# Attention and two expert layers in one program: where the first tile of the first layer is written in, and when the rest of w_out is decoded

## The chip, the cores and the metric

The kernel runs on one core of one Trainium2 chip. The metric is the device time of one execution, in microseconds (us). The engines are named as the profile names them: PE is TensorE, ACT ScalarE, DVE VectorE, POOL GpSimd, SP SyncE; each works through its own list of instructions, and semaphores tie the lists together.

## The reference

Three stages follow each other. The shapes are 4 batches, 8 heads, 768 positions, head size 64, so 3,072 tokens of 512 numbers, which leave the attention as `x`.

```python
# attention: 4 sink positions and a window of 128
scores = np.where(is_sink | in_window, scale * q @ k.T, -1e9)
attn = softmax(scores) @ v
# first MoE: w_in (512 x 1024), w_out (1024 x 512)
h = x @ w_in
solu = h * softmax(h)
ln = (solu - mean) / np.sqrt(var + 1e-6) * g_ln
x2 = ln @ w_out
# second MoE: 8 experts, the best one per token
e = argmax(x2 @ w_gate)
out[token] = gate[token] * (np.maximum(x2 @ w1[e], 0) @ w2[e])
```

## The kernel before, in words

**Tiles.** The attention is done in 32 units of two heads by 384 positions (`unit`, L153). Four units in a row hold all eight heads of 384 positions, which is a block of three tiles of 128 tokens; so units 0 to 3 feed tiles 0 to 2 of the first MoE, units 4 to 7 tiles 3 to 5, and so on to 24 tiles. A unit loads q and k (`a_load`), splits them into a high and a low float32r part (`a_split`: two copies on ACT at L179 and L180, two subtractions on POOL, nine copies by DMA at L187), makes six score matrices (`a_scores`: PE at L217 and L218, the mask and row maximum on DVE at L220, the exponential on ACT at L222), transposes them (`a_trans`, PE L270, ACT L271) and multiplies by v (`a_out`, PE L286 and L292). The result leaves PSUM as `bxh` (ACT, L297) and `bxl` (DVE, L298). The first three units use plain float32 and skip the split.

**The first MoE.** For each tile `m_in` makes two sums `h` of 12 matmuls each, three (L420 to L422) for each of the four 128-row chunks of w_in; chunk k reads unit k of the block. `m_act` then takes both sums through softmax and the normalisation: ACT at L437 (two), L445 (two), L448, L449 and L454, with small steps of DVE between. `m_tr` transposes (L469, ACT L472), `m_out` multiplies by w_out (L490 to L492) and writes the tile to DRAM. `moe1` (L530) has the tiles two deep: tile u goes in while tile u-2 goes out, and before the first `m_out` it asks for all of w_out (`yield ("wo", 0)`, L550).

**The weights.** w_in and w_out come as 64-bit float patterns and are decoded in 8 steps each (`decode`, L311): a DMA issued on ACT's queue (L314), two integer steps on DVE (`dt`, `dec`), two conversions on ACT (L321, and `dh` at L323), an addition on POOL (L324), a product on DVE (L325), then high and low part (ACT L362, DVE L363 for w_out). A w_out step also copies the block (ACT L366), transposes it on PE (L342, `wt`), copies it again (ACT L344, `xt`) and multiplies it by the gate weights (PE L350, `wt2`).

**PSUM.** `ps` (L78) hands out the eight banks of 128x512: three of them for the attention's `s`, `tp`, `skp` and `av`, five for the rest: `h`, `lt`, `x2`, `wt`, `wt2`, `dt`, `dh`. An `h` keeps its bank from its first matmul to its last reader, L445 of `m_act`.

**What sets the order.** Three generators are written into the program in turns: `ga` (attention), `gw` (weights) and `gm` (first MoE). First comes a loop that takes one step of the attention at a time, 110 of them (`C0`), and every sixth (`WSTEP`) one decode step: the eight of w_in first, and from step 62 on (`C1`) those of w_out.

```python
while done_x[0] < 0 or cnt_ < C0:                      # L1147
    step(ga, "a")
    cnt_ += 1
    ...
    if cnt_ % WSTEP == 0 and (wn[0] < 8 or C1 <= cnt_ and wn[0] < 16):
        step(gw, "w")
        wn[0] += 1
for _ in range(max(0, 16 - wn[0])):                    # L1155
    step(gw, "w")
    ...
```

Then a second loop (L1162) takes turns between the attention, while its written work is at most 0.7 (`RATIO`) of that of the first MoE, and one step of the first MoE; each second step of the MoE (`WSTEP2`) it takes one step of `gw`, if any is left. A unit is some 14 steps of the attention, and its output is written two units behind its scores: after 70 steps the scores of six units and the outputs of four are written, after 110 the scores of nine and the outputs of six. This written order is not yet that of the engines: the framework's scheduler goes over it and lists, for each engine, what it expects to be ready. So a matmul written later can stand earlier on PE than one written before it.

Of the kernel before, what the change touches and what calls it, by code (L numbers as in the profile page):

```python
# [37 lines left out]
XT = 21  # L38
WSB = 6
HG, HD, HSTEP, FH = 1, 5, 2, 2  # L40
C0, C1, WSTEP, WSTEP2, RATIO = 110, 62, 6, 2, 0.7
ROOM = [608, 576, 512, 416, 384, 320, 288, 128]
CAPS = [-(-n // 128) * 128 for n in ROOM]
NBLK = sum(CAPS) // 128
# [8 lines left out]
def body(ctx, tc, a):  # L53
# [476 lines left out]
    def moe1(nt):  # L530
        yield ("in", 0)
        m_x(0)
        for t in range(-LA, nt):
            u = t + LA
            if u < nt:
                yield from m_in(u, 0)
                if u + 1 < nt:
                    if (u + 1) % 3 == 0:
                        yield ("in", (u + 1) // 3)
                    m_x(u + 1)  # L540
            if t >= 0 and t != nt - 2:
                yield from m_tr(t)
            if u < nt:
                yield from m_in(u, 1)
                tin[0] = u + 1
                m_act(u)
            if t == nt - 3:
                yield from m_tr(t + 1, True)
            if t == 0:
                yield ("wo", 0)  # L550
            if t >= 0:
                yield from m_out(t, 128 * t, m_route(t - 1, tok_i[:, t - 1:t]) if t else ())
            if t == TE + 1:
                yield ("head", 0)
# [99 lines left out]
    def open_w():  # L654
        pool2["w"] = c_ctx.enter_context(tc.tile_pool(name="w2p", bufs=1, side="right"))
# [146 lines left out]
    def head():  # L802

        wq = []
        plan_head()
        for _ in range(HG):
            yield 0
        for c in range(4):
            w_fetch(0, 1, c)
        with tc.issue_after(loaded[-1].ins):  # L810
            load_ids(0, 0, HEAD)
        for _ in range(HD):
            yield 0
        x_gather(0, 0, HEAD)
        parts = [(which, c) for which in (1, 2) for c in range(4)]
        for n, p in enumerate(parts):
            if p == (2, 3):
                while not early_t:
                    yield 0
            if p[0] == 2 and p not in wq:  # L820
                w_fetch(0, *p)
            tc.keep_in_program_order(w_high(0, *p))
            if n < 3:
                w_fetch(0, 2, n)
                wq.append((2, n))
            yield 0
            tc.keep_in_program_order(w_low(0, *p))
            yield 0
        while len(late) <= XT:
            yield 0  # L830
        with tc.issue_after(late[XT].ins):
            for _ in x_trans(0, 0, HEAD):
                pass
# [275 lines left out]
    def weights():  # L1109
        yield from load_w_in()  # L1110
        yield from load_w_out()

    ga, gm, gw = attention(), moe1(NT), weights()
# [3 lines left out]
    def step(g, name):  # L1117

        y = hold.pop(name, None)
        if y is None:  # L1120
            y = next(g, None)
        if y is None:
            return None
        if isinstance(y, tuple):
            kind, b = y
            if kind == "x":
                done_x[0] = b
            elif kind == "head":
                assert not a_open
                open_w()  # L1130
                gh[0] = head()
            elif kind == "wo":
                while step(gw, "w") is not None:
                    pass
            elif kind == "w" and tin[0] < b:
                hold[name] = y
                return 0
            elif kind == "in":
                if done_x[0] < b:
                    hold[name] = y  # L1140
                    return 0
                done_in[0] = b
            return 1e-6
        return max(y, 1e-6)

    cnt_, wn = 0, [0]
    while done_x[0] < 0 or cnt_ < C0:  # L1147
# [4 lines left out]
        if cnt_ % WSTEP == 0 and (wn[0] < 8 or C1 <= cnt_ and wn[0] < 16):  # L1152
            step(gw, "w")
            wn[0] += 1
    for _ in range(max(0, 16 - wn[0])):  # L1155
        step(gw, "w")
        wn[0] += 1
    ta = tm = 0.0
    mcnt = 0
    gh = [None]  # L1160
# [81 lines left out]
```

## Time and profile before

| what | before |
|---|---|
| median of 3 runs | 844.85 us (836.87 to 855.21) |
| the profiled execution, its own time | 840.65 us |
| its span, first to last instruction | 838.9 us |
| PE busy | 787.2 us, 94% of the span |
| ACT, DVE, POOL busy | 495.1, 489.7, 383.4 us |
| mean granted clock of PE | 0.983 of full |

The profile is of one execution. Its span leaves out 1.75 us of its own time. A busy PE is pipelined: a matmul's row overlaps the next, so the price of one in a row of many is the distance between starts. Windows give, for a stretch of the span, how long each engine was busy, and the clock that PE was granted. A wait names the engine that waited, and what ended the wait.

### The profile page before, as it was taken

Reading aid. Unit: us, or ns where it says so; the run is one execution under the profiler, and the core shown is the slowest. Engines: PE = TensorE matmul, PEld = TensorE weight load, DVE = VectorE, ACT = ScalarE, POOL = GpSimd, SP = SyncE. Lnnn points to the kernel's source line nnn. Section 1 sums busy time; section 2 is a strip of 40 time slices with the busy share of each in tenths; the row PEclk is TensorE's granted clock in tenths of the full one; section 3 lists DMA queues with packets and bytes.
Section 4 is the critical chain, followed back from the end, with each engine's and each line's share of the span. In section 5 each row is a group of like instructions: output and inputs, shape, how many; then the busy total and the mean of one; then the engine's idle time right before and its main releaser. Section 6 shows DMA issues by size and latency. Waiting matters only on the chain.

```text
span 838.9 us, 15049 instructions
## 1 busy us (share of the span) xinstructions
PE 787.2 (94%) x4946; PEld 685.3 (82%) x4946; DVE 489.7 (58%) x1606; ACT 495.1 (59%) x1236; POOL 383.4 (46%) x418
## 2 busy tenths in 40 slices
PE   2667999999999999999999989999999999999996
PEld 1246878988788888888888879889988898989985
DVE  6977777787587776767675575435314242434430
ACT  4788787877568777777775464244324252544541
POOL 4877755464355455545432021157225262635531
PEclk9998899999999999999999999999999999999998
DMA  7688555677665565566420271277325253536410
GB/s 263 196 223 212 140 149 139 92 166 122 118 166 118 126 158 128 135 152 113 119 28 28 36 242 35 69 255 242 95 91 191 88 187 101 181 122 200 150 57 17
DMA packets 77383, 114.34 MB, mean 136 GB/s; under 512 B 14125, under 2 KB 53485, under 8 KB 77296
## 3 DMA queue, kind: packets, MB, share of 16 engines
q1 hardware_dynamic: 69744, 91.02, 43.1%
q0 software_dynamic: 5248, 13.88, 4.7%
q10 hardware_dynamic: 2304, 8.39, 3.2%
q8 instruction: 41, 0.67, 0.4%
q14 instruction: 46, 0.38, 0.3%
HBM read 72.22 MB, written 13.94 MB: 103 GB/s over the span
## 4 chain that ended last, share of the span: by engine, by line
PE 77%; DMA 11%; issue 4%; DVE 3%; ACT 3%; POOL 1%; POOLq 0%; SPq 0%; ACTq 0%; DVEq 0%
PE x L490 5%; PE x L492 5%; PE ht L770 5%; PE x L491 5%; PE ht L771 5%; PE ht L772 5%; PE h L420 5%; PE h L422 5%; PE h L421 5%; PE y L792 5%; PE y L791 5%; PE y L790 5%; PE av L292 4%; PE s L217 3%; PE s L218 2%
## 5 line engine op out<-in xcount | busy, mean ns | idle before, releaser
L222 ACT ACTIVATE P<-P,mx 128x272 f32<-128x272 f32 x192 | 98.7, 515 | 30.4 <-DVE mx L220 29.3
L490 PE MATMUL x<-woh,lh 128*128 128x256 f32 (+1 forms) x384 | 112.2, 292 | 0.4 <-DVE ll L473 0.4
L492 PE MATMUL x<-woh,ll 128*128 128x256 f32 (+1 forms) x384 | 110.7, 289 | 0.0
L491 PE MATMUL x<-wol,lh 128*128 128x256 f32 (+1 forms) x384 | 109.7, 286 | 0.0
L220 DVE CUSTOM_DVE_ANT_0 P<-s,mk 128x272 f32<-128x272 f32 x192 | 81.0, 435 | 36.6 <-PE s L218 34.2
L694 POOL TENSOR_TENSOR wl<-wst,wh 128x1024 fp32r<-128x1024 f32 x28 | 68.3, 2438 | 64.1 <-ACT wh L688 63.9
L688 ACT ACTIVATE wh<-wst 128x1024 fp32r<-128x1024 f32 x64 | 67.5, 1058 | 47.1 <-PE ht L771 35.5
L771 PE MATMUL ht<-xel,wh 128*128 128x288 f32 (+6 forms) x288 | 90.0, 314 | 0.0
L772 PE MATMUL ht<-xeh,wl 128*128 128x288 f32 (+6 forms) x288 | 89.8, 313 | 0.0
L790 PE MATMUL y<-wh,hh 128*128 128x512 f32 x224 | 89.6, 401 | 0.0
L770 PE MATMUL ht<-xeh,wh 128*128 128x288 f32 (+6 forms) x288 | 88.5, 313 | 0.0
L792 PE MATMUL y<-wh,hl 128*128 128x512 f32 x224 | 88.1, 395 | 0.0
L791 PE MATMUL y<-wl,hh 128*128 128x512 f32 x224 | 87.6, 392 | 0.0
L694 DVE TENSOR_TENSOR wl<-wst,wh 128x1024 fp32r<-128x1024 f32 x36 | 55.6, 1552 | 50.7 <-ACT wh L688 50.7
L420 PE MATMUL h<-wih,bxh 128*128 128x512 f32 x192 | 78.8, 410 | 0.0
L421 PE MATMUL h<-wil,bxh 128*128 128x512 f32 x192 | 76.9, 401 | 0.0
L422 PE MATMUL h<-wih,bxl 128*128 128x512 f32 x192 | 76.7, 400 | 0.0
L490 PEld LDWEIGHTS x<-woh,lh 128*128 128x128 f32 x384 | 73.0, 190 | 1.3 <-DVE ll L473 0.5
L797 ACT ACTIVATE y<-y,gate 128x512 f32<-128x512 f32 x28 | 19.3, 689 | 92.8 <-PE y L792 73.5
L491 PEld LDWEIGHTS x<-wol,lh 128*128 128x128 f32 x384 | 73.1, 190 | 0.7 <-issue 0.2
L492 PEld LDWEIGHTS x<-woh,ll 128*128 128x128 f32 x384 | 73.2, 191 | 0.6 <-issue 0.3
L774 DVE SCALAR_TENSOR_TENSOR hl<-ht,hh 128x288 fp32r<-128x288 f32 (+6 forms) x80 | 38.3, 491 | 57.5 <-ACT hh L773 57.2
(229 smaller groups left out, 2067.2 us busy)
## 6 DMA issues: line engine op xcount, KB each, us to landing
wst<-w SPq DMA_DIRECT2D x64, 512.0 KB, 3.9
x_d<-xrow SPq DMA_DIRECT2D x24, 264.0 KB, 6.2
qd<-qT SPq DMA_DIRECT2D x32, 192.0 KB, 3.5
qB<-qA SPq DMA_DIRECT2D x58, 96.0 KB, 3.2
lB<-lA SPq DMA_DIRECT2D x58, 96.0 KB, 2.6
kd<-kx SPq DMA_DIRECT2D x16, 280.0 KB, 3.3
w<-w_in ACTq DMA_DIRECT2D x8, 512.0 KB, 7.5
w<-w_out ACTq DMA_DIRECT2D x8, 512.0 KB, 4.5
```

What stands on the lines that cost most here:

```text
L420: T.matmul(h, xh[k], wih[:, k, cs], start=(k == 0), stop=False)
L421: T.matmul(h, xh[k], wil[:, k, cs], start=False, stop=False)
L490: T.matmul(p[:, 0:n], lh[:, k, :], woh[:, k, c, 0:n], start=(k == 0), stop=False)
L491: T.matmul(p[:, 0:n], lh[:, k, :], wol[:, k, c, 0:n], start=False, stop=False)
L492: mm = T.matmul(p[:, 0:n], ll[:, k, :], woh[:, k, c, 0:n], start=False, stop=(k == 7))
L694: return (G if c % 2 and r else V).tensor_tensor(out=l_, in0=st_w.pop((r, which, c)), in1=raw(h_), op=ALU.subtract)
L770: T.matmul(o, wh[:, k, fs], xh(k), start=(k == 0), stop=False)
L771: T.matmul(o, wh[:, k, fs], xl(k), start=False, stop=False)
L772: T.matmul(o, wl[:, k, fs], xh(k), start=False, stop=(k == 3))
L790: T.matmul(o, hh[:, k, sl], wh, start=(k == 0), stop=False)
L791: T.matmul(o, hh[:, k, sl], wl, start=False, stop=False)
L792: T.matmul(o, hl[:, k, sl], wh, start=False, stop=(k == 7))
```

## The change

`C0` goes from 110 to 70, so the second loop begins behind the output of unit 3, some four units earlier, and the loop that wrote what was left of the 16 decode steps ahead of it is gone. With 70 steps only the first step of w_out is written in the first loop; the other seven are written in the second, one at every second step of the first MoE, all within its first two tiles.

```diff
-C0, C1, WSTEP, WSTEP2, RATIO = 110, 62, 6, 2, 0.7
+C0, C1, WSTEP, WSTEP2, RATIO = 70, 62, 6, 2, 0.7
...
             wn[0] += 1
-    for _ in range(max(0, 16 - wn[0])):
-        step(gw, "w")
-        wn[0] += 1
     ta = tm = 0.0
```

**PE behind unit 0's output.** In the fences below a row is one instruction, or several equal ones; numbers behind the names tell tiles apart, and they are counted in written order, so the same number need not be the same tile in both programs. `av_419` is unit 0's output in both. Before, from there on:

```order
L292 MATMUL av_419<-pt_310,vd_256 64x128 x2
L217 MATMUL s_456<-kA_404,qA_400 128x272
L218 MATMUL s_456<-kA_404,lA_402 128x272
L342 MATMUL wt_837<-ident_78,dec_790 128x128 x4
L217 MATMUL s_461<-kB_405,qB_401 128x272
L218 MATMUL s_461<-kB_405,lB_403 128x272
L217 MATMUL s_479<-kA_404,qA_400 128x272
L218 MATMUL s_479<-kA_404,lA_402 128x272
L217 MATMUL s_484<-kB_405,qB_401 128x272
L218 MATMUL s_484<-kB_405,lB_403 128x272
```

and with the change:

```order
L292 MATMUL av_419<-pt_310,vd_256 64x128 x2
L217 MATMUL s_456<-kA_404,qA_400 128x272
L218 MATMUL s_456<-kA_404,lA_402 128x272
L217 MATMUL s_461<-kB_405,qB_401 128x272
L218 MATMUL s_461<-kB_405,lB_403 128x272
L420 MATMUL h_817<-wih_68,bxh_441 128x512
L421 MATMUL h_817<-wil_69,bxh_441 128x512
L342 MATMUL wt_836<-ident_78,dec_790 128x128 x4
L217 MATMUL s_479<-kA_404,qA_400 128x272
L218 MATMUL s_479<-kA_404,lA_402 128x272
L422 MATMUL h_817<-wih_68,bxl_442 128x512
```

The first sum of the first tile (`h_817`) now begins right behind unit 0's output. Before, the first L420 stands behind unit 4's output. The six matmuls of the first sum that read units 0 and 1 stand before unit 2's output now, and its last behind the scores that follow unit 3's.

**PE between the outputs of unit 5 and unit 6.** `av_1086` before and `av_1243` with the change are unit 5's. Before:

```order
L286 MATMUL av_1086<-skt_849,vsk_361 128x384 x2
L292 MATMUL av_1086<-pt_874,vd_802 64x128 x2
L292 MATMUL av_1086<-pt_874,vd_802 64x256 x4
L292 MATMUL av_1086<-pt_874,vd_802 64x128 x2
L350 MATMUL wt2_1301<-wg_sb_121,xt_1299 128x8 x4
L420 MATMUL h_1361<-wih_68,bxh_441 128x512
L421 MATMUL h_1361<-wil_69,bxh_441 128x512
L422 MATMUL h_1361<-wih_68,bxl_442 128x512
L420 MATMUL h_1361<-wih_68,bxh_560 128x512
L421 MATMUL h_1361<-wil_69,bxh_560 128x512
L217 MATMUL s_1139<-kA_1071,qA_1067 128x272
```

and with the change:

```order
L286 MATMUL av_1243<-skt_856,vsk_361 128x384 x2
L292 MATMUL av_1243<-pt_916,vd_802 64x128 x2
L292 MATMUL av_1243<-pt_916,vd_802 64x256 x4
L292 MATMUL av_1243<-pt_916,vd_802 64x128 x2
L350 MATMUL wt2_1200<-wg_sb_121,xt_1146 128x8 x4
L342 MATMUL wt_1207<-ident_78,dec_1132 128x128 x4
L217 MATMUL s_1321<-kA_1228,qA_1224 128x272
L218 MATMUL s_1321<-kA_1228,lA_1226 128x272
L217 MATMUL s_1326<-kB_1229,qB_1225 128x272
L218 MATMUL s_1326<-kB_1229,lB_1227 128x272
L217 MATMUL s_1334<-kA_1228,qA_1224 128x272
L218 MATMUL s_1334<-kA_1228,lA_1226 128x272
```

Before, 48 matmuls of L420 to L422 stand between the outputs of units 5 and 6; with the change none does. Counted over PE's list, before the outputs of units 4, 5 and 6 stand 0, 12 and 60 of these matmuls in the program before, and 36, 48 and 48 in the changed one; of the eight transposes of w_out (L342) 6, 8 and 8 before, and 4, 6 and 8 in the changed one; and before unit 6's output all eight L350 groups of four stand in the program before, and seven in the changed one.

**ACT up to the copy of unit 6.** `bxh_1313` before and `bxh_1417` with the change are unit 6's. Before:

```order
L449 ACTIVATE sc_1359<-sc_1359 128x1
L222 ACTIVATE P_1136,sm_1138<-P_1136,mx_1137 128x272
L271 ACTIVATE pt_1213<-tp_1214 128x3x128
L271 ACTIVATE pt_1213<-tp_1219 128x3x128
L445 ACTIVATE h_1445,sc_1495<-e_1571,sc_1495 128x512
L445 ACTIVATE h_1497,sc_1495<-e_1571,sc_1495 128x512
L297 ACTIVATE bxh_1313<-av_1245 128x384
L454 ACTIVATE e_1426<-e_1426,sc_1359 128x1024
```

and with the change:

```order
L448 ACTIVATE sc_1179<-sc_1179 128x1
L222 ACTIVATE P_1318,sm_1320<-P_1318,mx_1319 128x272 x2
L271 ACTIVATE pt_1374<-tp_1375 128x3x128
L271 ACTIVATE pt_1374<-tp_1380 128x3x128
L449 ACTIVATE sc_1179<-sc_1179 128x1
L344 ACTIVATE xt_1261<-wt_1256 128x512
L454 ACTIVATE e_1280<-e_1280,sc_1179 128x1024
L297 ACTIVATE bxh_1417<-av_1406 128x384
```

The L454 that ends tile 0's normalisation stands behind the copy of unit 6 before; now both tile 0's and tile 1's stand ahead of it. Counted over ACT's list from the copy of unit 0 to that of unit 6, the changed program has two L454, one L448, one L449 and two L323 more, one more DMA issue (L314), and is otherwise the same, instruction for instruction.

## Rows read from the trace of the kernel before

**Rows 1.** The page: span, TensorE's busy share, and the span in 40 slices.

```profile
span 838.9 us, 15049 instructions
...
PE 787.2 (94%) x4946; PEld 685.3 (82%) x4946; DVE 489.7 (58%) x1606; ACT 495.1 (59%) x1236; POOL 383.4 (46%) x418
...
PE   2667999999999999999999989999999999999996
PEclk9998899999999999999999999999999999999998
```

**Rows 2.** Busy time by stretch; first line: the columns (PEclk: granted clock).

```profile
core 0: us, PE busy (x) PEld busy (x) DVE busy (x) ACT busy (x) POOL busy (x), PEclk, DMA share, GB/s
50.88:92.70 41.82, 32.28 (x195) 25.94 (x196) 31.70 (x97) 36.61 (x97) 31.86 (x34) 0.80 0.79 205
92.70:119.77 27.07, 26.82 (x171) 22.33 (x171) 20.75 (x70) 19.27 (x58) 14.97 (x19) 1.00 0.53 132
50.88:119.77 68.89, 59.10 (x365) 48.27 (x365) 52.45 (x166) 55.88 (x155) 46.83 (x52) 0.88 0.69 177
143.84:196.00 52.16, 52.16 (x366) 46.23 (x365) 41.31 (x151) 40.20 (x120) 25.61 (x28) 1.00 0.75 123
196.00:220.00 24.00, 20.47 (x142) 17.35 (x141) 14.16 (x53) 14.03 (x41) 11.82 (x16) 0.93 0.69 127
```

**Rows 3.** The timeline of ScalarE: copies of units 0, 4 and 6.

```profile
50.88 0.49 ACT L297 ACTIVATE bxh<-av 128x384 fp32r<-128x384 f32 x1 [1.14 <-PE s L218]
92.70 0.49 ACT L297 ACTIVATE bxh<-av 128x384 fp32r<-128x384 f32 x1
119.77 0.47 ACT L297 ACTIVATE bxh<-av 128x384 fp32r<-128x384 f32 x1
```

**Rows 4.** The timeline of TensorE: the first tile's start, before unit 5.

```profile
start us, us, engine line op out<-in xcount [idle before <-releaser]
92.58 1.06 PE L350 MATMUL wt<-wg_sb,xt 128*128 128x8 f32 x8
93.50 0.64 PE L342 MATMUL wt<-ident,dec 128*128 128x128 f32 x4
93.89 0.48 PE L420 MATMUL h<-wih,bxh 128*128 128x512 f32 x1
...
95.17 0.39 PE L420 MATMUL h<-wih,bxh 128*128 128x512 f32 x1
95.41 0.39 PE L421 MATMUL h<-wil,bxh 128*128 128x512 f32 x1
95.64 0.39 PE L422 MATMUL h<-wih,bxl 128*128 128x512 f32 x1
```

**Rows 5.** Groups by line, ScalarE, whole span; the time behind | is busy.

```profile
L454 ACT ACTIVATE e<-e,sc 128x1024 f32<-128x1024 f32 x24 | 29.7, 1239 | 11.7 <-DVE sc L453 11.7
L323 ACT ACTIVATE dh<-w 128x512 f32<-128x512 f32 x16 | 10.1, 629 | 0.0
L449 ACT ACTIVATE sc<-sc 128x1 f32<-128x1 f32 x24 | 4.7, 194 | 0.2
L448 ACT ACTIVATE sc<-sc 128x1 f32<-128x1 f32 x24 | 4.6, 192 | 0.5 <-DVE sc L447 0.3
```

**Rows 6.** Waits of ScalarE from 46 to 110 us.

```profile
engine line waited for: us in total, times, longest us
ACT woh L362 <- DVE dh L325: 3.4, 2, 2.0
ACT w L321 <- DMA w<-w_out: 3.3, 4, 1.8
```

**Rows 7.** Waits of VectorE from 46 to 110 us, same columns.

```profile
DVE dt L318 <- ACT xt L344: 2.3, 2, 1.9
```

**Rows 8.** Waits of TensorE from 119.77 us to the end, same columns.

```profile
PE s L218 <- DMA lA<-lA: 3.5, 2, 2.0
```


## The prediction

> **What bounds the kernel now.** I read the page first. PE is busy 94% of the span, and in the row of slices it is short of full only in the first four of 40, each 21 us long, and in the last; its granted clock is under nine tenths in the fourth, the fifth and the last [rows 1]. So behind some 110 us the kernel is a row of matmuls, and what the change can win or lose is decided ahead of that. The windows tell what that stretch is like [rows 2]. I set their marks at the copies of units 0, 4 and 6 on ACT, at 50.88, 92.70 and 119.77 us [rows 3], because the order of the change can be counted at the same marks. From unit 0 to unit 4 PE is busy 32.28 of 41.82 us, at a mean clock of 0.80, and ACT 36.61 of 41.82, which is 87.5%, more than any other engine. From unit 4 to unit 6 it is the other way round: PE 26.82 of 27.07 us, ACT 19.27, or 71%. From 143.84 to 196.00 PE has no gap at all: 52.16 of 52.16. The reader is to see two phases: a start in which ACT sets the pace, and PE has 9.5 us to spare, and then PE alone. The first L420 starts at 93.89 us [rows 4], where the phases meet.
>
> **What the change moves, and its price.** The matmuls of tiles 0 and 1 go from behind unit 4 into the first phase: 36 of them stand ahead of unit 4's output, where none stood. Their price is the distance of their starts, 95.17 to 95.41 to 95.64, or 0.235 us each [rows 4], so 8.5 us in all, against 9.5 us that PE stood idle there [rows 2]. At first sight that is a gain of 8.5 us. But what was taken from the second phase is not replaced: between units 4 and 6 the changed order has 12 of these matmuls in place of 60, and no other MoE work, only scores and late decode steps. So the second phase becomes one in which PE waits, and the question is when unit 6 is reached.
>
> That I take from ACT's list, since its contents between the copies of units 0 and 6 differ by so little. It was busy 55.88 us of 68.89 there [rows 2]. Added are two L454 at 1.239 us, two L323 at 0.629, one L448 at 0.192 and one L449 at 0.194 [rows 5]: 2.48 + 1.26 + 0.39 = 4.1 us, so 60.0 us. (A DMA issue more on ACT's queue I count as nothing: its own row is not busy time.) How long 60.0 us of work take depends on how well ACT is fed, for which the rows give three rates. At 100%, which no stretch shows, 60.0 us: unit 6 comes 8.9 us sooner. At the 87.5% of the first phase, 68.6 us: 0.3 us sooner. At the 81.1% of the whole stretch (55.88 of 68.89), 74.0 us: 5.1 us later. I take 87.5%, because the whole stretch from unit 0 to unit 6 now looks like the first phase did, with decode steps, scores and PE in gaps.
>
> Against that stands what PE has done by then. Ahead of unit 6's output the changed list has 12 matmuls of L420 to L422 fewer (48 in place of 60), 12 x 0.235 = 2.8 us, and one group of L350 fewer. The profile has each such group as eight rows; one takes from 92.58 to 93.50, so 0.9 us [rows 4]. Behind unit 6 PE is full, so those 3.7 us are owed. The three rates give -8.9 + 3.7 = -5.2, -0.3 + 3.7 = +3.4 and +5.1 + 3.7 = +8.8 us.
>
> The remaining edits: the seven decode steps written later are the same instructions. Before unit 4's output stand four transposes in place of six, and all eight are done by unit 6, long before the first L490, so the request for all of w_out costs nothing; were it late, the first L490 would wait with all of PE behind it. Seven loads of w_out are written later on ACT's queue; ACT waited 3.3 us for such loads, in four waits [rows 6], which is inside the 87.5%. POOL (46.83 of 68.89) and DVE (52.45) have room [rows 2]. SP's copies for the split are the same ones in a moved order, and one later stall hangs on their landing: from 196 to 220 us PE lacks 3.5 us, waiting for `lA` [rows 2, 8], and runs at a mean clock of 0.93, another 0.07 x 24 = 1.7 us. The changed program meets that place with its transfers shifted, so it can be spared the 5.2 us, meet them again, or meet them twice: I take once, and keep -5.2 and +5.2 for the range. Behind unit 31 both orders have nearly the same work left (504 matmuls of L420 to L422 are through in both), so the second MoE moves as a block.
>
> The sum is made against the profiled execution's own 840.65 us: 840.65 + 3.4 = 844.05, say 844. That execution lies 4.2 us under the median of the three runs, 844.85; by the median the sum would be 848.3. I keep 844 and let the range hold the other.
>
> **A rule for the clock.** In the first phase the clock was 0.80 with PE idle 23% of the time; in the second it was 1.00 with PE full [rows 2]. The Trainium skill ("TensorE: Matmul & The Clock Gate", section "Why this matters for your kernels") asks for no idle gaps between bursts of matmuls, as PE falls to the half level behind one. By that rule the 36 matmuls in the gaps would hold the clock at 2.4 GHz, and up to 0.20 x 41.82 = 8.4 us come back: 844.05 - 8.4 = 835.7. I do not take it, because ACT was the fuller engine in that stretch and a faster PE does not feed it more than 100%.
>
> **Rival one, a gain.** PE has matmuls between the scores, its clock stays up, scores come sooner, and ACT loses its gaps. For it: 1.14 us of waiting for PE just at the first copy [rows 3], and that the first phase was paced by nobody fully. Against it: 3.3 us of ACT's gaps were w_out loads [rows 6], and a score now stands behind matmuls that want a `bxh` just made. At ACT's limit it gives 840.65 - 5.2 = 835.4. That is also where the rule for the clock ends up, so the two share a chance.
>
> **Rival two, slower.** A sum `h` that begins behind unit 0 holds its bank until L445, behind unit 3. The first tile's two sums lie open from unit 1 to unit 3, so two of the five banks outside the attention are gone, and `dt`, `dh`, `wt` and `wt2` of each decode step take turns in three. In the rows such turns show already with five: DVE waited with `dt` for ACT's reading of `wt` 2.3 us in two waits, 1.15 each [rows 7], and ACT waited with `woh` for `dh` 3.4 us in two, 1.7 each [rows 6]. If all seven late decode steps pay both, 7 x 2.85 = 20 us fall on ACT, the engine that sets the pace: 844.05 + 20 = 864. It is slower by 2% (857.5) from 1.9 us a step on. Against it: seven steps in 68.9 us are one in 10 us, and the banks it needs are free most of that. What makes such a wait dear is what stands behind it. The Trainium skill ("PSUM — Partial Sum Buffer", section "Engine vs sequencer instructions") has the queues of ScalarE and VectorE as strictly first in, first out; by that rule each of these waits holds the exponentials and masks behind it too, and the 864 stands.
>
> **Rival three, no effect.** The order shows that the tiles do move, so the change does what it says; but with ACT at 60.0 of 65.2 us, 92%, what is won up to unit 6 and the 3.7 us owed cancel: 840.65.
>
> **How the numbers follow.** The forecast, ACT at 80 to 90%, has 0.45; rival three 0.2; rival one 0.25; rival two 0.1. Most of this lies close together: -5.2 to +8.8 us, and with the later stall once less or once more -10.4 to +14.0, so 830 to 855; the median's 4.2 us widen the upper end to 858. A difference of 2% (17 us) is about what a measurement of this kernel can tell from no change. Faster by more than that needs rival one, the spared stall and 6 us that I see nowhere: 0.04. Slower needs rival two, or the forecast's 81% with the stall met twice and more: 0.1. Within 2%: 0.86.
>
> **What would show it.** In the changed profile the first L420 should start near 52 us, behind the first copy on ACT. The seventh copy should start 68.6 us behind the first: 60 us would prove rival one, 74 or more rival two or a loss of pace. ACT should be busy 60 us between them. PE should have its gaps between the copies of units 4 and 6 now, some 9 us of them where there were 0.25 (26.82 busy, less 48 x 0.235, plus one group of L350 at 0.9 and two of L342 at 0.39 [rows 4], is 17.2 of some 27 us), and fewer ahead of unit 4. If PE is full through both phases, I am wrong about ACT. If DVE's `dt` and ACT's `dh` or `woh` wait for banks in five steps or more, rival two is at work. If the L490 of the first tile waits for `wol` or `woh`, the cover over the decode was thinner than I counted.

## The result, and the profile after

The changed kernel took 851.73 us in the median of four runs (849.26 to 855.53), the kernel before 844.07 us beside it (836.87 to 855.21): a ratio of 1.0108, interval 1.0063 to 1.0153. A later repeat on another chip gave 1.0154 (1.0127 to 1.0182). So it is 8 to 13 us slower, where the forecast was 3.4 us slower. The profiled execution, the slowest of the four, took 855.53 us, 14.9 us more than that of before. The page of the changed kernel:

```profile
span 853.7 us, 15061 instructions
...
PE 794.3 (93%) x4946; PEld 689.4 (81%) x4946; DVE 498.3 (58%) x1606; ACT 495.2 (58%) x1236; POOL 386.8 (45%) x418
...
PE   2667789999999999999999989999999999999996
PEclk9998879999999999999999999999999999999998
```

PE's fifth and sixth slices (some 85 to 128 us) were 9 and 9 and are 7 and 8 now, and the granted clock is low up to the sixth [rows 1]. Behind that PE's row is 9 but for one slice of 8 and the last, as before. The timeline of ScalarE, copies of units 0, 1, 2, 3, 4, 5 and 6:

```profile
50.40 0.49 ACT L297 ACTIVATE bxh<-av 128x384 fp32r<-128x384 f32 x1 [0.58 <-PE av L292]
58.81 0.49 ACT L297 ACTIVATE bxh<-av 128x384 fp32r<-128x384 f32 x1
74.65 0.51 ACT L297 ACTIVATE bxh<-av 128x384 fp32r<-128x384 f32 x1
85.03 0.51 ACT L297 ACTIVATE bxh<-av 128x384 fp32r<-128x384 f32 x1
104.13 0.48 ACT L297 ACTIVATE bxh<-av 128x384 fp32r<-128x384 f32 x1
116.73 0.50 ACT L297 ACTIVATE bxh<-av 128x384 fp32r<-128x384 f32 x1
131.61 0.49 ACT L297 ACTIVATE bxh<-av 128x384 fp32r<-128x384 f32 x1 [0.29 <-PE av L292]
```

Unit 0 is where it was; unit 4 came at 92.70 and comes at 104.13, unit 6 at 119.77 and now 131.61 [rows 3]. The worst piece is from unit 3 to unit 4: 19.1 us. Busy time by stretch (columns as in [rows 2]); the last row is from 30 us to the copy of unit 8:

```profile
50.40:104.13 53.73, 41.04 (x230) 31.79 (x230) 37.06 (x109) 38.31 (x103) 34.88 (x37) 0.87 0.68 173
104.13:131.61 27.48, 23.57 (x120) 18.77 (x120) 18.85 (x64) 21.44 (x60) 15.55 (x18) 0.69 0.43 114
50.40:131.61 81.21, 64.61 (x350) 50.56 (x350) 55.91 (x171) 59.76 (x161) 50.42 (x54) 0.81 0.60 153
85.03:104.13 19.10, 15.02 (x84) 12.50 (x84) 16.39 (x45) 13.29 (x36) 9.66 (x12) 0.85 0.61 150
...
30.00:163.68 133.68, 108.85 (x612) 85.37 (x613) 92.44 (x284) 97.16 (x263) 77.03 (x82) 0.89 0.57 150
```

and the same last stretch, to unit 8's copy, of the kernel before:

```profile
30.00:143.84 113.84, 95.87 (x575) 75.56 (x575) 86.60 (x268) 92.27 (x254) 77.49 (x84) 0.93 0.67 174
```

Three things are to be seen. ACT did what was counted: 59.76 us of work from unit 0 to unit 6, against 60.0 in the prediction. But it took 81.21 us over it, 73.6%. And no engine is full in either phase any more: from unit 4 to 6, where PE was full at full clock, it is busy 23.57 of 27.48 us at a mean clock of 0.69.

The last two rows give a measure for all that follows. Behind unit 8 PE is nearly full, so what counts ahead of it is the time that PE did not use, as gaps or at half clock: the stretch less busy time times mean clock. Before: 113.84 - 95.87 x 0.93 = 24.7 us. After: 133.68 - 108.85 x 0.89 = 36.8 us. The difference, 12.1 us, is most of the 14.9. Nearly all of it, 11.0 us, lies from unit 4 to unit 6: 27.48 - 23.57 x 0.69 = 11.2 us, against 27.07 - 26.82 x 1.00 = 0.25 before [rows 2]; up to unit 4 the loss grew by only 2.0 us (18.0 against 16.0).

The waits from unit 0 to 6 (us in total, times, longest), first of ScalarE, then of VectorE, then of TensorE:

```profile
ACT w L321 <- DMA w<-w_out: 5.6, 3, 2.5
ACT woh L362 <- DVE dh L325: 5.3, 3, 2.7
ACT P L222 <- DVE mx L220: 4.3, 6, 1.3
```

```profile
DVE P L220 <- PE s L218: 10.4, 6, 6.0
DVE woh L353 <- PE wt L350: 3.7, 3, 3.0
...
DVE dt L318 <- ACT dec L366: 0.7, 1, 0.7
```

```profile
PE s L217 <- DVE mx L220: 5.9, 6, 2.5
PE s L218 <- DMA lA<-lA: 2.2, 1, 2.2
```

ACT waits for DVE and for loads, DVE for PE, PE for DVE: each list waits for another. From unit 4 to unit 6 alone, where the loss lies, PE's longest waits are for DVE's masks:

```profile
PE s L217 <- DVE mx L220: 4.7, 3, 2.5
```

### The profile page after: what moved, and what is told of

The parts are those of the page before. It is cut to its first block, busy times and chain, and to the rows that moved or that the text cites. A ratio compares the mean times of both kernels' runs of the same rounds, so it can differ in the third digit from the quotient of the medians.

```text
span 853.7 us, 15061 instructions
## 1 busy us (share of the span) xinstructions
PE 794.3 (93%) x4946; PEld 689.4 (81%) x4946; DVE 498.3 (58%) x1606; ACT 495.2 (58%) x1236; POOL 386.8 (45%) x418
## 4 chain that ended last, share of the span: by engine, by line
PE 71%; DMA 10%; DVE 9%; issue 5%; ACT 3%; POOL 1%; SPq 1%; POOLq 0%; ACTq 0%; DVEq 0%
PE ht L770 5%; PE ht L771 5%; PE ht L772 5%; PE x L490 5%; PE y L792 5%; PE y L791 5%; PE y L790 5%; PE x L492 5%; PE x L491 4%; PE h L420 4%; PE h L422 4%; PE h L421 4%; PE av L292 4%; PE s L217 2%; DMA w<-w_out 2%
## 5 line engine op out<-in xcount | busy, mean ns | idle before, releaser
L490 PE MATMUL x<-woh,lh 128*128 128x264 f32 (+1 forms) x384 | 112.0, 292 | 0.4 <-DVE ll L473 0.4
L492 PE MATMUL x<-woh,ll 128*128 128x264 f32 (+1 forms) x384 | 110.3, 287 | 0.0
L491 PE MATMUL x<-wol,lh 128*128 128x264 f32 (+1 forms) x384 | 109.7, 286 | 0.0
L182 POOL TENSOR_TENSOR lA<-qd,qA 128x384 fp32r<-128x384 f32 x29 | 29.4, 1015 | 114.3 <-ACT qA L180 83.1
L420 PE MATMUL h<-wih,bxh 128*128 128x512 f32 x192 | 79.3, 414 | 0.4 <-ACT bxh L297 0.4
L422 PE MATMUL h<-wih,bxl 128*128 128x512 f32 x192 | 76.4, 401 | 0.4 <-DVE bxl L298 0.4
L490 PEld LDWEIGHTS x<-woh,lh 128*128 128x128 f32 x384 | 72.7, 189 | 1.7 <-issue 0.7
L797 ACT ACTIVATE y<-y,gate 128x512 f32<-128x512 f32 x28 | 19.3, 689 | 92.5 <-PE y L792 73.3
```

The source lines that it names most:

```text
L420: T.matmul(h, xh[k], wih[:, k, cs], start=(k == 0), stop=False)
L490: T.matmul(p[:, 0:n], lh[:, k, :], woh[:, k, c, 0:n], start=(k == 0), stop=False)
L491: T.matmul(p[:, 0:n], lh[:, k, :], wol[:, k, c, 0:n], start=False, stop=False)
L492: mm = T.matmul(p[:, 0:n], ll[:, k, :], woh[:, k, c, 0:n], start=False, stop=(k == 7))
```

## The experiments

Ratios are to the kernel before, in runs on the same chip, with their 95% intervals. "PE's loss" is the measure above, from 30 us to the copy of unit 8 (24.7 us before, 36.8 after), from each run's own windows. Where an expectation counts decode steps ahead of a unit on PE, it counts the groups of L342 and of L350 together, so 16 groups for the eight steps of w_out; 11 of them stand ahead of unit 4's output before, 8 with the change.

### Which of the two edits

The change with the loop that writes the rest of the decode put back, so that only the first tile moves (e1):

```diff
+    for _ in range(max(0, 16 - wn[0])):
+        step(gw, "w")
+        wn[0] += 1
```

> The first tile is written behind 70 steps, but all of w_out is still decoded ahead of it (the loop that wrote the rest of the decode steps is kept). In PE's list no sum of the first tile then begins before unit 4's output, as in the program before, and by unit 6 there are 72 matmuls of L420 to L422 in place of 60. Theory one (the place of the decode: steps written behind the first tiles draw the decode out, and let sums begin early that hold PSUM banks): this costs nothing, ratio to before 0.993 to 1.003, and unit 6's copy follows unit 0's by 66 to 71 us. Theory two (the attention's lead: four units less ahead, PE comes to wait for it): ratio 1.007 to 1.015, with unit 6 as early as before and PE's gaps behind it.

The late decode without the early tile (e2), the change at half the distance (e4), and the change once more (e5):

```diff
-C0, C1, WSTEP, WSTEP2, RATIO = 70, 62, 6, 2, 0.7
+C0, C1, WSTEP, WSTEP2, RATIO = 110, 108, 6, 2, 0.7   # e2
+C0, C1, WSTEP, WSTEP2, RATIO = 90, 62, 6, 2, 0.7     # e4
```

> The first tile is written behind 110 steps, as before, but only the first step of w_out is decoded ahead of it and the other seven between its steps (C0 110, C1 108, no loop). PE's list up to unit 6's output is then that of the changed kernel, nearly row for row, while the attention's written lead is that of before. Theory one (the place of the decode): ratio to before 1.006 to 1.015, unit 6's copy 76 to 82 us behind unit 0's. Theory two (the lead): ratio 0.997 to 1.004.

> The change with 90 steps in place of 70: five of the eight steps of w_out are decoded ahead of the first tile, three between its steps. The first sum begins behind unit 2's output. Theory one (the place of the decode): a third of the late decode is left, ratio 0.998 to 1.005. Theory two (the lead): half of the shorter lead, 1.004 to 1.008.

> The changed kernel once more, for a second profile and more times on the chip of the other three. Both theories: ratio to before 1.006 to 1.015. The profile of the change had unit 6's copy 81.2 us behind unit 0's, and its run was the longest of four; if that is chance, this one shows 75 to 78 us, with ACT busy some 60 us of it again.

Measured: e1 840.91 us, 1.0055 (1.0027 to 1.0084); e2 846.95, 1.0153 (1.0116 to 1.0190); e4 842.84, 1.0097 (1.0064 to 1.0131); e5 848.64, 1.0154 (1.0127 to 1.0182). PE's loss: e1 29.9, e2 32.2, e4 27.7, e5 37.1 us. The early tile alone costs a third of the loss, the late decode alone all of it; the two do not add. Of the expectations, theory one holds for e2 and both miss for e1 and e4: e4 is slower than either wanted, and e1 lies between them, though its unit 6 comes 80.7 us behind unit 0, as late as in the change. PE had done 72 matmuls of L420 to L422 by then in place of 48, so a late unit 6 is not by itself the loss. Nor does PE's loss tell all: for e4 it accounts for 3.0 of some 8 us, and where the rest lies stays open. The order of e2 tells why it is as slow as the change: up to unit 7 PE's list has the same counts of sums and decode steps ahead of each unit as the changed one (36 matmuls of L420 to L422 ahead of unit 4's output). Once the decode is written late, the sums stand as early with 110 steps as with 70, so the scheduler pulls them forward by itself. The repeat shows the same shape, 81.3 us from unit 0 to 6.

### Loads of w_out one step ahead

```diff
...
-        w = dec_p[0].tile([128, 512, 2], I32, tag="w64", name="w64", bufs=WB)
-        A.dma_start(out=w, in_=src)
+        while nf[0] < min(16, i + 2):
+            wq.append(dec_p[0].tile([128, 512, 2], I32, tag="w64", name="w64", bufs=WB)); A.dma_start(out=wq[-1], in_=srcs(nf[0])); nf[0] += 1
+        w = wq.pop(0)
...
```

> The changed kernel, with each load of a decode step issued one step ahead, so that its data lie there when ACT comes to L321; the three buffers and the order of the steps are as before. In the changed kernel ACT waited 5.6 us in three waits for w_out between units 0 and 6, up to 2.5 us at a time and 5 us in the later repeat, and the chain passes through two of them. Theory A, the chain through the queues (every wait on ACT's list holds the exponentials, the transposes' copies and the split behind it): these waits are gone, units 0 to 6 take some 76 in place of 81 us, and the kernel stands 7 to 9 us above the one before in place of 13. Theory B, the banks: ACT then waits for dh or wt in the same places, the stretch stays at 79 to 82 us and the kernel 11 to 13 us above. If it stands within 3 us of the one before, the late loads were the whole loss.

Measured: 847.00 us, 1.0110 (1.0079 to 1.0142); units 0 to 6 in 77.9 us, PE's loss 34.7. ACT's waits for w_out stay, 5.1 us in three: the edit did not move the loads. ACT's list from unit 0 on is that of the change, and the issue that came at 86.68 us comes at 85.91. So the run is nearly a repeat, and says nothing on what the loads cost.

### The banks

The kernel before with two banks held from unit 0 to unit 3 (f3; it computes four small things more, which nobody reads), and both kernels with two banks for the attention and six for the rest (`PA = 3` to `PA = 2`):

```diff
+        if not hogs and len(x_t.get(0, [])) == 1:
+            hogs = [ps("h"), ps("h")]
+            for h in hogs:
+                T.matmul(h[:, 0:128], raw(x_t[0][0][1])[:, 0:128], ident, start=True, stop=True)
+        if len(hogs) == 2 and len(x_t.get(0, [])) == 4:
+            for h in hogs:
+                V.tensor_tensor(out=const.tile([128, 1], F32, tag="hog", name="hog"), in0=h[:, 0:1], in1=raw(x_t[0][3][1])[:, 0:1], op=ALU.add)
+            hogs.append(0)
```

> The kernel before with two banks of the five outside the attention taken behind unit 0's output (two small matmuls into them) and given back behind unit 3's output (two small adds), and no first tile in between. It adds four small instructions to the computation, whose results nobody reads. Its order then has 3 decode steps in place of 11 ahead of unit 4's output, and no L420 there. Theory A, chain: with little else in the lists the bare attention steps fast, 7 us a unit or less, so units 0 to 4 take under 34 us in place of 41.8. Theory B, banks (the waits come from the two banks alone): units 0 to 4 take as long as in the changed kernel or nearly, 48 us or more, with waits for dt, dh and wt. The whole is slower than before in either case by 5 to 15 us, since eight decode steps and 46 matmuls move behind unit 4.

> The changed kernel with two of the eight PSUM banks for the attention in place of three, so six in place of five for the decode and the first MoE. Its order has all sixteen decode steps and 60 of L420 to L422 through ahead of unit 4's output. To be read against the same edit on the kernel before. Theory B, banks (the two open sums leave the decode too few): with a sixth bank the change costs little, this one is within 4 us of its control. Theory A, chain: the sums and steps still stand among the attention's instructions, this one is 8 us or more behind its control. Against the kernel before I expect it anywhere from 10 us faster (PE's matmuls fill the start) to 15 us slower (the attention with two banks steps slower, as each score waits for a mask to be done).

> The control: the kernel before with two banks for the attention and six for the rest. All sixteen decode steps are through ahead of unit 3's output in its order, and 60 of L420 to L422 ahead of unit 4's. Theory B: 5 us faster to 5 us slower than before, since here the banks were not short. Theory A: slower by 5 to 15 us, since the attention's chain loses a bank and gets more in front of it.

Measured: f3 856.21 us, 1.0214 (1.0182 to 1.0246); units 0 to 4 in 46.7 us, with `dt` waiting 0.7 us in two. Both theories missed: the bank waits were not there, and the attention was not fast, because the decode of w_in, done ahead of unit 0 before, now fell into these units too (unit 0 came at 40.98 us). With six banks 914.28 us (1.0883) after and 915.31 us (1.0924) before: the two are alike, as theory B wanted, but they are 75 us slower than the kernel before, and most of that lies behind unit 8 (PE's loss up to there is 31.7 us after and 36.3 before), so the difference between them was measured in another program. What the banks do shows in the orders: with six, all 16 groups of the decode and 60 matmuls of L420 to L422 stand ahead of unit 4's output, in place of 8 and 36 with the change and 11 and none before. Waits that look like turns for a bank (`dt` for ACT's last reading) come to 0.7 us in f3 and 0.7 us in the changed kernel.

### The split of q and k

Scores of units 3 to 6 without the split, on the changed kernel (g1) and on the one before (g2):

```diff
-NATP = 3
+NATP = 7
```

> The changed kernel with the scores of units 3 to 6 computed from the loaded q and k as they are (as units 0 to 2 are), without the split: no kA, qA, lA and none of the nine copies on SP for these units; everything else is the changed kernel. Theory A, chain: the stretch to unit 6 is long because the split (ACT, then POOL, then nine copies, then the next scores) is queued behind decode and sum work. Then units 0 to 6 take 70 us or less in place of 81, and the kernel comes to within 4 us of the one before. Theory B, banks or plain work: ACT loses eight copies (some 3 us of 59.8) and the stretch stays at 77 us or more, the kernel 8 to 13 us above the one before.

> The control for the run without the split in units 3 to 6: the same edit on the kernel before. Theory A, chain: here too the split is a part of the chain, units 0 to 4 take 36 us or less in place of 41.8, and the kernel is 3 to 8 us faster than the one before. Theory B: the start is paced by ACT's work, which loses some 3 us, and the time moves by 0 to 3 us.

Measured: g1 840.49 us, 1.0028 (1.0004 to 1.0053), PE's loss 26.3 us; g2 841.23, 1.0050 (1.0027 to 1.0073). Without split and copies most of the change's loss is gone, as theory A wanted, though unit 3 to 4 still takes 19.5 us in g1 and units 0 to 6 take 77.2, as theory B wanted. In the kernel before the same edit costs 3.5 us, against both expectations: there PE is busy 86.15 of the 87.48 us from unit 0 to 6, at a mean clock of 0.84. What a plain float32 score costs PE beside a split one was not measured by itself. So the split takes part in the loss, but is not all of it.

### More work for ACT

```diff
             A.activation(out=x, in_=p, func=AF.Copy)
+            A.activation(out=x, in_=p, func=AF.Copy)
```

> The changed kernel with the copy L366 of each w_out decode step done twice (the same result): 8 more ACT instructions of 0.6 us, 4.8 us, seven of them between units 0 and 6. If ACT's throughput paces the stretch (87.5% as in the prediction), the stretch grows by 4.2 / 0.875 = 4.8 us or more. If the stretch is paced by the serial chain of several in-order lists (theory A), it grows by about as much, 3 to 6 us, since ACT's list is one of the chain's. If the banks or PE pace it, ACT with 26% idle hides it: 0 to 1.5 us over the changed kernel's 8 to 13 us.

> The control: the kernel before with L366 done twice, 4.8 us more for ACT, nearly all of it ahead of unit 5. If ACT at 87.5% paces the start (the prediction's reading), the kernel is 4 to 6 us slower. If no single engine paces it, 1 to 4 us.

Measured: after 843.17 us, 1.0051 (1.0021 to 1.0081), before 840.58, 1.0029 (1.0000 to 1.0058). With eight ACT instructions more the changed kernel is faster than without them. From unit 0 to 6 it takes 70.0 us, and from unit 4 to 6:

```profile
99.39:120.20 20.81, 18.85 (x116) 13.97 (x117) 18.80 (x59) 19.16 (x53) 14.34 (x18) 0.92 0.55 150
```

ACT is busy 92% there and DVE 90%, where the changed kernel has 78% and 69%. The edit moves the order as well (36 matmuls of L420 to L422 ahead of unit 5's output in place of 48, and 13 groups ahead of unit 6's in place of 15), and that is the point: ACT's throughput was not what held the changed kernel at 73.6%. In the kernel before the same copies lengthen units 0 to 6 by 6.2 us, more than ACT's share at 87.5% would. But units 0 to 3, where ACT's work is the same (27.5 us against 27.9), take no longer, and all of it lies from unit 3 to 4 (17.2 us against 10.3). ACT has 4.1 us more to do there, but is busy only 75%, and these two rows of PE and DVE stand in it:

```profile
81.47 0.59 PE L218 MATMUL s<-kA,lA 128*128 128x272 f32 x1 [2.67 <-DMA lA<-lA]
82.11 0.44 DVE L220 CUSTOM_DVE_ANT_0 P<-s,mk 128x272 f32<-128x272 f32 x1 [5.39 <-PE s L218]
```

That stall will be met again below; with it this kernel is 0.3% slower (1.0029), some 2 us.

### The attention alone, and the kernel before again

The chunks of each sum in another order, so that no sum can begin before unit 3's output (e3):

```diff
-        for k in range(4):
-            T.matmul(h, xh[k], wih[:, k, cs], start=(k == 0), stop=False)
+        ks = (3, 0, 1, 2)
+        for k in ks:
+            T.matmul(h, xh[k], wih[:, k, cs], start=(k == ks[0]), stop=False)
             T.matmul(h, xh[k], wil[:, k, cs], start=False, stop=False)
-            T.matmul(h, xl[k], wih[:, k, cs], start=False, stop=(k == 3))
+            T.matmul(h, xl[k], wih[:, k, cs], start=False, stop=(k == ks[3]))
```

> The changed kernel with the four chunks of each sum of L420 to L422 in the order 3, 0, 1, 2, so that a sum can't begin before unit 3's output is there. In its order there is nothing but attention between the outputs of units 0 and 3 on PE and ACT (no decode step, no L420), and 12 matmuls and one step ahead of unit 4's. Theory A, chain: the bare attention takes 7 us a unit or less there, so units 0 to 3 come in 21 us or less (31.6 before, 34.6 after), and what is put among it lengthens it one for one. If the attention alone is already at 9 us a unit or more, its own chain sets the pace and the rest cost little in those gaps. As a whole it is the slowest of the four, 15 to 30 us above the kernel before, since decode and sums then follow one another behind unit 4.

> The kernel before, once more with a profile: whether the 41.8 us from unit 0 to unit 4, the 68.9 to unit 6 and the 24.7 us of PE time lost up to unit 8 are what it always does. I expect 41 to 46, 68 to 73 and 24 to 28 us. If they lie near the changed kernel's 53.7, 81.2 and 36.8, the profile of before was a lucky one and the comparison of the starts falls.

Measured: e3 854.51 us, 1.0206 (1.0168 to 1.0245). With nothing but attention units 0 to 3 take 23.25 us, 7.7 us each, between the two expectations; with nine groups of the decode among them (before) 31.6, with five groups and 18 matmuls (after) 34.6. So what stands among the attention does lengthen the start, by some 2 us a step of two groups (8.3 us for nine), and no engine is full even without it (PE 18.37 of 23.25 us, POOL 19.03, ACT 16.64). The kernel before, once more: 838.34 us, 1.0006 (0.9983 to 1.0029), 42.2 us to unit 4, 69.3 to unit 6, PE's loss 25.2. So its short start comes again, and so does the change's loss by this measure: 37.1 - 25.2 = 11.9 us.

### Amount or order

The late decode steps at every step of the first MoE (f5), at every fourth (f4), at every third (l2), and at every second but one step sooner (l1). For all of them the sums begin as early as in the change.

```diff
-C0, C1, WSTEP, WSTEP2, RATIO = 70, 62, 6, 2, 0.7
+C0, C1, WSTEP, WSTEP2, RATIO = 70, 62, 6, 1, 0.7     # f5; 4 in f4, 3 in l2
...
-        if mcnt % WSTEP2 == 0:
+        if mcnt % WSTEP2 == 1:                           # l1
```

> The changed kernel with a late decode step written behind every step of the first MoE in place of every second. Its order has 24 matmuls of L420 to L422 and 11 steps' transposes ahead of unit 4's output (36 and 8 in the changed kernel), and 60 and 16 ahead of unit 6's (48 and 15). If the loss comes from sums that are open while decode steps still want banks and places, it shrinks with their number: 4 to 8 us above the kernel before, units 0 to 6 in 70 to 76 us, and PE loses 2 to 5 us between units 4 and 6 in place of 11. If it comes from the matmuls being early at all, 10 us or more.

> The changed kernel with a late decode step behind every fourth step of the first MoE. Its order has 48 matmuls and 5 steps ahead of unit 4's output, 60 and 11 ahead of unit 6's, and no L420 at all between units 5 and 7. By the same reason the loss grows or stays: 13 to 20 us above the kernel before, with PE losing 12 us or more between units 4 and 8. If instead the decode is free where PE would be full, and only its number in the start counts, this one is faster than the changed kernel: 5 to 9 us above the one before.

> The changed kernel with the late decode steps written behind every second step of the first MoE as there, only one step sooner (the odd ones in place of the even). Its order has the same 3, 12, 18, 36 and 48 matmuls of L420 to L422 ahead of the outputs of units 1 to 5, and two steps more of the decode ahead of each. Theory O, the order alone (who stands directly in front of a score, a mask or an exponential on the in-order lists): with as much work in the start or more, it can lose much less; I expect units 0 to 6 in 68 to 78 us and the kernel 2 to 9 us above the one before. Theory W, amount (each sum and each decode step among the attention costs its own time): two steps more make it as slow as the changed kernel or slower, 11 to 16 us above, units 0 to 6 in 80 us or more.

> The changed kernel with a late decode step behind every third step of the first MoE (every first, second and fourth gave 3.3, 8 to 13 and 0.2 us above the kernel before). Theory O: no trend, anything from 0 to 10 us; units 0 to 6 in 65 to 78 us. A smooth law with its worst at every second step would give 5 to 9 us, and the amount of late decode in the start (theory W: fewer steps ahead of unit 4's output, 7 against 8 and 5) 4 to 8 us.

| run | ratio (interval) | ahead of unit 4: L420 to L422 / L342 and L350 groups | unit 0 to 6, us | PE's loss, us |
|---|---|---|---|---|
| before | 1 | 0 / 11 | 68.9 | 24.7 |
| the change, repeat | 1.0154 (1.0127 to 1.0182) | 36 / 8 | 81.3 | 37.1 |
| f5, every step | 1.0039 (1.0013 to 1.0065) | 24 / 11 | 72.6 | 23.6 |
| l1, one step sooner | 1.0023 (0.9994 to 1.0053) | 36 / 10 | 72.0 | 24.5 |
| l2, every third | 0.9998 (0.9971 to 1.0025) | 48 / 7 | 69.3 | 24.0 |
| f4, every fourth | 1.0004 (0.9978 to 1.0030) | 48 / 5 | 66.7 | 25.8 |

Theory W falls with l1: as many matmuls as in the change and two groups more ahead of unit 4, and a fifth of the loss or less. It falls with l2 too, for which it wanted 4 to 8 us. The expectation that f4 would lose more than the change fell too. What stands among the attention has its price in the start, as e3 shows, but it need not be lost in the whole: four neighbours of the change, with early sums and a late decode like it, lose 0 to 3 us in all. So the 8 to 13 us hang on the order of the change (and of e2, whose counts ahead of each unit are the same), not on the amount that it moves. e4, a neighbour at another distance, loses some 8 us too.

Part of what the order costs can be read by setting unit 3 to 4 of the change beside l1, which has the same 18 matmuls and three groups between them, and takes 11.88 us in place of 19.10. Its row:

```profile
82.86:94.74 11.88, 11.28 (x71) 8.78 (x71) 11.54 (x34) 10.44 (x29) 9.28 (x10) 1.00 0.58 152
```

PE and DVE are nearly full (95% and 97%), at full clock. By PE's loss the stretch costs 0.6 us here and 6.3 in the change, nearly half of the 12.3 us by which the two differ up to unit 8. In the changed kernel it begins with a stall. SyncE's timeline there:

```profile
76.09 0.59 SPq L187 DMA_DIRECT2D lB<-lA  x1
76.73 0.59 SPq L163 DMA_DIRECT2D qd<-qT  x1
80.44 0.33 SPq L164 DMA_DIRECT2D kd<-kx  x1
80.89 0.47 SPq L187 DMA_DIRECT2D qB<-qA  x1
82.08 0.47 SPq L187 DMA_DIRECT2D lA<-lA  x1
```

and its wait ahead of the load of k:

```profile
SPq L164 <- DMA kA<-kd: 3.0, 1, 3.0
```

The last of the nine copies, `lA`, stands behind the loads of the next q and k, and the load of k waited 3.0 us for a buffer that a copy was still reading. In l1 `lA` stands ahead of that load:

```profile
76.18 0.47 SPq L187 DMA_DIRECT2D lA<-lA  x1
76.75 0.53 SPq L164 DMA_DIRECT2D kd<-kx  x1
```

What hangs on it, in the changed kernel, on PE, DVE and ACT:

```profile
82.80 0.39 PE L217 MATMUL s<-kA,qA 128*128 128x272 f32 x1 [1.42 <-ACT pt L271]
85.37 0.60 PE L218 MATMUL s<-kA,lA 128*128 128x272 f32 x1 [2.17 <-DMA lA<-lA]
```

```profile
86.11 0.44 DVE L220 CUSTOM_DVE_ANT_0 P<-s,mk 128x272 f32<-128x272 f32 x1 [6.03 <-PE s L218]
...
93.69 0.69 DVE L318 TENSOR_SCALAR dt<-w 128x512 int32<-128x512 int32 x1 [0.72 <-ACT dec L366]
94.29 0.15 DVE L435 TENSOR_TENSOR sc<-sc 128x1 f32<-128x1 f32 x1
94.42 0.69 DVE L320 SCALAR_TENSOR_TENSOR dec<-w,dt 128x512 int32<-128x512 int32 x1
95.02 0.68 DVE L426 TENSOR_REDUCE sc<-h 128x1 f32<-128x512 f32 x1
95.62 0.43 DVE L220 CUSTOM_DVE_ANT_0 P<-s,mk 128x272 f32<-128x272 f32 x1
```

```profile
81.71 0.66 ACT L321 ACTIVATE w<-w 128x512 int32<-128x512 uint32 x1 [2.49 <-DMA w<-w_out]
...
86.59 0.52 ACT L222 ACTIVATE P<-P,mx 128x272 f32<-128x272 f32 x1 [1.06 <-DVE mx L220]
86.68 0.34 ACTq L314 DMA_DIRECT2D w<-w_out  x1
...
92.51 0.67 ACT L321 ACTIVATE w<-w 128x512 int32<-128x512 uint32 x1 [1.68 <-DMA w<-w_out]
93.07 0.59 ACT L366 ACTIVATE dec<-dh 128x512 f32<-128x512 f32 x1
```

Read from the top: ACT waits 2.49 us for a load of w_out, and PE 1.42 us for the copy `pt` behind it in ACT's list; then PE waits 2.17 us for `lA`. DVE stands idle 6.03 us for that score, ACT for DVE's mask, and the next load of w_out, which is behind that exponential in ACT's list, is issued only at 86.68 and takes to 92.5. With it L321 is late, behind it L366, behind that DVE's `dt`, and behind `dt`, `dec` and L426 stands the mask of a score of the next unit. Each is a wait of 0.7 to 6 us, and each list hands it on.

That this stall is the loss is not shown, and several traces speak against it as the whole. In the kernel before `lA` stands behind the load of k as well, which waited 3.2 us there, and PE came to that score later than `lA`:

```profile
77.22 0.33 SPq L164 DMA_DIRECT2D kd<-kx  x1
78.42 0.47 SPq L187 DMA_DIRECT2D lA<-lA  x1
```

The kernel before with more work for ACT meets the stall itself, 2.67 us of PE and 5.39 us of DVE, and loses some 2 us; in f5 PE waits 2.97 us for `lA`, and f5 loses 0.4%. Unit 3 to 4 stays long in g1 without any split, and e4 loses some 8 us though DVE never waits more than 0.7 us for a score of L218 between its units 0 and 6. A kernel that moves `lA` alone was not run. What is shown is that as much early work in another order loses 0 to 3 us in place of 8 to 13; which places of the order cost how much stays open, and most of PE's loss against the kernel before lies behind this stretch, from unit 4 to unit 6.

No version beat the kernel before; l1, l2 and f4 cannot be told from it.

## Why the prediction was wrong

**The step that failed** is the rate: "I take 87.5%, because the whole stretch from unit 0 to unit 6 now looks like the first phase did". ACT's 60.0 us of work would have taken 68.6 us; its 59.76 us took 81.2, 73.6%, under even the lowest rate that I drew from the rows, 81.1%. With the measured time the sum comes near: unit 6 comes 81.21 - 68.89 = 12.3 us later, the 3.7 us owed make it 16.0, and the profiled executions differ by 14.9. One term of it was not the program's: the later stall, 5.2 us from 196 to 220 us, is not in the repeat of the kernel before (PE busy 24.00 of 24.00 us there, clock 1.00), and in the changed program PE lacks 1.3 us from 200 to 240. With that counted the sum is 16.0 - 3.9 = 12.1.

**Why it was a poor step.** I read 87.5% as the mark of an engine that sets the pace, and so as a property of the phase, which would stay when the order changes. It did not stay: from unit 0 to 4 ACT's rate went from 87.5 to 71.3% (38.31 of 53.73 us), and with eight ACT instructions more the changed kernel lost less (1.0051 in place of 1.0108 to 1.0154), with a rate from unit 0 to 6 of 82% (57.45 of 69.99 us) in place of 73.6. The Trainium skill ("Perfetto Trace Analysis", section "Identifying the Most-Contended Engine") would have begun as I did: it takes the engine with the highest occupancy as the bottleneck. Here the measurement differs, as that engine had room. In the start of the kernel before, beside ACT, DVE stood at 76%, POOL at 76%, PE at 77% of the first phase and the DMA engines at 0.79 [rows 2]; one order gave ACT 87.5% from unit 0 to 4, another 71.3.

**The gaps of PE.** "8.5 us in all, against 9.5 us that PE stood idle there" put the early matmuls into PE's gaps in thought. The gaps stayed: 41.82 - 32.28 = 9.5 us up to unit 4 before, 53.73 - 41.04 = 12.7 after. They are waits for other lists. That each early matmul also delays the score behind it fits the longer start (34.6 us for units 0 to 3, 23.3 in e3), but was not measured by itself.

**What held.** The first L420 starts at 50.95 us, near 52 as forecast. ACT's work held (59.76 us), the matmuls and the group behind the 3.7 us owed (48 and seven ahead of unit 6's output), and the cover over the decode: no wait of the first L490, at 140.62 us, shows in the trace. PE's loss did move behind unit 4, but not as forecast: its gaps there are 3.9 us in place of some 9, and the half clock, which the forecast left out, makes it 11.2.

**The rivals.** Rival one and the rule for the clock fell. Up to unit 4, where the matmuls went in, the clock rose a little (0.80 to 0.87; in the repeats 0.76 and 0.84) but did not reach full speed, and unit 4 came later, not sooner; from unit 4 to 6 it fell from 1.00 to 0.69. Rival two came nearest to the size, not to the place: `woh` waited for `dh` 5.3 us in three, `dt` once for 0.7, so bank waits in five steps or more are not there. But its sentence on what stands behind a waiting instruction is what the trace shows. Rival three fell with the rate. Of the forecast's range, 830 to 858, the median is inside; the likeliest value was 8 us too low.

## What to carry to other kernels

When four engines and the DMA queues stand at 76 to 88% together, as in this start, do not take the highest share for a rate that stays, nor the idle time of another engine for gaps that can be filled: here both came out of how in-order lists wait for each other, and changed with the order. Before a change that reorders such a phase, bound its pace from the bare chain (here 7.7 us a unit) up to well under the lowest rate seen, and look in the new order for what stands directly in front of each score, mask and last copy. And when a knob only moves places, run its neighbours before judging the idea: here the value tried was the worst of the five places tried for the late decode.

## What the runs showed of the hardware

From unit 4 to 6 PE went to the half clock in a stretch in which it was busy 86%. The timeline of TensorE in the changed kernel:

```profile
104.23 0.39 PE L217 MATMUL s<-kA,qA 128*128 128x272 f32 x1 [1.80 <-DVE mx L220]
...
110.12 0.63 PE L420 MATMUL h<-wih,bxh 128*128 128x512 f32 x1
110.55 0.63 PE L421 MATMUL h<-wil,bxh 128*128 128x512 f32 x1
...
111.63 0.40 PE L421 MATMUL h<-wil,bxh 128*128 128x512 f32 x1
111.87 0.40 PE L422 MATMUL h<-wih,bxl 128*128 128x512 f32 x1
```

Behind a gap of 1.80 us before 104.23 and one of 0.53 us before 105.35 a matmul of L420 to L422 starts 0.43 us ahead of the next (1.2 GHz) up to 111, and 0.24 us (2.4 GHz) in the rest of the twelve. I had priced such matmuls at 0.235 us each; half of these cost nearly twice that. The Trainium skill ("TensorE: Matmul & The Clock Gate", section "Why this matters for your kernels") warns of a fall to the half level behind idle gaps between matmuls. The rows agree with the fall, though the gaps here are shorter than those that it names; what the fall takes off the time is in PE's loss above and was not measured by itself.
